# One attention and mixture kernel: float16 state products in every batch, keys scaled into a spare tile, weight words fetched a step early, products of a chunk pair three side steps later

## The chip, the cores and the metric

One core of one Trainium2 chip runs the whole program. The metric is device time in microseconds, from the program's start to its end. The kernel before took 1023.17 us in the median of three runs (1021.74 to 1024.06). Everything about time in this text comes from those runs and from one profiled execution of 1023.83 us.

## The reference

Four batches, 768 positions, 384 features (8 heads of 48). Three stages follow each other:

```python
# 1. attention: per head a complex decay a, normalised to a length under 1
a = a * min(|a|, 0.999) / (|a| + 1e-6)
S[t] = a[t] * S[t-1] + k[t] v[t]^T           # complex state, 48 x 48 per head
y[t] = q[t] . Re(S[t])
# 2. first feed-forward layer
u = x + (U V applied along the sequence)      # rank 32
x = u + relu(u @ w1) @ w2                     # 384 -> 1536 -> 384
# 3. second feed-forward layer
u = x + Re(fft over sequence and features of x)
un = layernorm(u)
x = u + relu(un @ w1') @ w2'
```

All results are float32, and the kernel keeps near that precision by splitting operands: a product of float32 accuracy is made of three products of a high and a low part (high x high, high x low, low x high).

## The kernel before, in words

**Attention.** A batch is cut into six chunks of 128 positions, taken in three pairs. `decays` and `turns` work elementwise on a pair (logarithm, running sums, sine and cosine) and write for each chunk a tile `QK` of turned queries and keys, position on the partitions. Six DMAs on SP's queue (L427) carry `QK` to `QT`, feature on the partitions. `products` then works on a chunk in small steps: the scores `sc` from `QT` (L452, TensorE, float32), the masked scores `pm` (VectorE, L457), the transposes `kp` of the keys from `QK` (L466), their split into `kh` and `kl` (L475, L476), the sum `y` (L484), the state's increment `g` (L484), and the new state `S` (L563 to L583). `g` is the product of keys and values of the chunk; `S` is scaled by `fe`, the decay over the chunk.

Two kinds of chunk exist. In the plain ones (all of batch 0, the first four of batch 1) keys are copied whole into `ke` (ScalarE, L471), and `y` and `g` are float32 products; `g` takes 16 products of 128 x 64 and 128 x 32 weights, 32 instructions in the profile. In the others values and keys are split into float16 parts (`vh`, `vl`, `kh`, `kl`), and `g` is 24 float16 products. In those chunks the keys are scaled by the decay before they are transposed: three in-place activations on `QK` (L509), after the DMAs have read it.

**First layer.** `moe_units(0)` goes over 4 batches x 2 groups of 384 positions x 12 slices `f` of the hidden features. A slice is nine products into `hp` (L92 to L94), `hh` on ScalarE (L179), the low part `hl` on VectorE (L181), and nine products into `acc`, those for the slice before. The weights come as 64-bit words: `load_w` fetches them (`stw`, L120), ScalarE and VectorE rebuild float32 numbers (`wxw`, L109 to L127) and split them (`w`, L138, L139).

**What runs beside what.** Attention of batch 0 stands alone, with the weights of the first layer woven in (`first_attention`). While batch b is in the first layer, `Side(attention(b+1), total, 40)` does the steps of the next batch's attention: 40 side slots share `total` steps evenly. In `attention`, each pair's products run zipped with the elementwise steps of the next pair. The second layer (`moe_units(1)`) follows with the Fourier part beside it.

**Order.** The program hands instructions to a scheduler that lays each engine's own order down by modelled readiness and by priority (`urgent`, `tc.high_priority`); on the chip each engine then goes strictly in its order. `warm` (L1001) are products whose result nobody uses, put behind given instructions: 20 behind the first scores, 4 behind the first and 4 behind the last of the products into `z`.

Of the kernel before, what the change touches and what calls it, by code (L numbers as in the profile page):

```python
# [23 lines left out]
NC = 6  # L24
# [10 lines left out]
IM_MOST = 0.96  # L35

# [6 lines left out]
def mixer_kernel(ctx, tc, a_in, qk_in, v_in, u_in, v4_in, w_in, cc_in, ss_in, cb_in, sb_in, id_in, mask_in, rows_in, out):  # L43
# [69 lines left out]
    def from_f64(src, name):  # L113
# [5 lines left out]
        st = moe.tile([128, 384, 2], I32, tag="u", name=f"st{name}", bufs=5)[:, :n]  # L119
        nc.sync.dma_start(st.rearrange("p n w -> p (n w)"), src.bitcast(I32))  # L120
# [11 lines left out]
    def load_w(mi, f, z):  # L132
# [4 lines left out]
        x = from_f64(w_in[mi, f][:, zs], f"w{mi}_{f}_{z}")  # L137
# [119 lines left out]
    def decays(m):  # L257
# [4 lines left out]
        def mk(nm):  # L262
            return at(f"{nm}{b}_{cc[0]}")

        if b == 0:
            if m == 2:
                turn = at(f"turn{b}_{cc[0]}", "turn", 1, (128, 2, 3, 2, 128))
                s1, s2 = turn[:, 0], turn[:, 1]
            else:
                s1, s2 = mk("L"), mk("s")  # L270
            T_ = a[:, 1]
            qf, kf = qk[:, 0], qk[:, 1]
        else:
            turn = at(f"turn{b}_{cc[0]}", "turn", 1, (128, 2, 3, 2, 128))
            T_, s1, s2 = turn[:, 1], mk("L"), mk("s")
# [5 lines left out]
        ew[m] = T_, Th, qf, kf, ends, a if b == 0 else turn  # L281
# [90 lines left out]
    def turns(m):  # L372
# [3 lines left out]
        T_, Th, qf, kf, ends, turn = ew[m]  # L376
# [6 lines left out]
        for js in jj:  # L383
# [31 lines left out]
            for j in range(js.start, js.stop):  # L415
# [12 lines left out]
                qkt[b, c] = QT, QK  # L428
                yield

    def products(m, j):
# [11 lines left out]
        QT, QK = qkt[b, c]  # L443
# [19 lines left out]
        def turned(z):  # L463
            kp.append(bank(f"kp{n}_{z}", pool)[:, :384])
            for i in range(3):
                T.transpose(kp[z][:, i * 128 : (i + 1) * 128], QK[:, z, i, 128:256], ident)  # L466

        def split(z):
            src = kp[z].rearrange("t (x h) -> t h x", h=8)
            if plain:  # L470
                A.copy(ke[:, :, z, :], src)  # L471
                return
            dh = kh[:, :768].rearrange("t (h z x) -> t h z x", h=8, z=2)[:, :, z, :]
            dl = kl[:, :768].rearrange("t (h z x) -> t h z x", h=8, z=2)[:, :, z, :]
# [29 lines left out]
        if not last:
            fe = t3("fe", 2, (96, 8))
            G.tensor_scalar(fe, QT[:, :, 256], 1.0 if plain and c == 0 else 1.0 / FSCALE, 0.0, ALU.mult, ALU.add)
            if not plain:
                for i in range(3):
                    A.activation(QK[:, :, i, 128:256], QK[:, :, i, 128:256], AF.Copy, scale=QK[:, 0, i, 256:257])  # L509
# [749 lines left out]
```

## Time and profile before

| | |
|---|---|
| runs, median of 3 | 1023.17 us (1021.74 to 1024.06) |
| profiled execution | 1023.83 us |
| its span | 1022.1 us |
| mean granted TensorE clock | 0.944 |
| TensorE products / VectorE / ScalarE / GpSimd busy | 86% / 64% / 46% / 23% |

The profile is of one execution. PE is TensorE (products), PEld its weight loads, DVE VectorE, ACT ScalarE, POOL GpSimd, SP the engine whose queue issues the DMAs. A granted clock of 1.00 is 2.4 GHz and of 0.50 is 1.2 GHz. By the first `hh` (L179) of each batch the span falls into: attention of batch 0 up to 147.4 us; first layer of batch 0 to 319.9, of batch 1 to 453.1, of batch 2 to 575.6, of batch 3 to 681.2; second layer to the end.

### The profile page before, as it was taken

How to read it: one execution, taken by the hardware profiler on the slowest of the kernel's cores; microseconds unless marked ns; L12 is line 12 of the kernel's file. 1: busy time of each engine (PE TensorE's matmuls, PEld its weight loads, DVE VectorE, ACT ScalarE, POOL GpSimd, SP SyncE). 2: the span in 40 equal slices, each digit the busy share in tenths (PEclk: the TensorE clock that was granted, in tenths of full speed). 3: DMA queues.
4: the chain of work that ended last, by engine and by line, in shares of the span. 5: the costliest groups of instructions: out<-in, count | busy, mean ns of one | idle time of the engine just before them, and what ended most of it. 6: DMA issues, size and time to landing. Idle time of an engine off the chain costs nothing.

```text
span 1022.1 us, 16249 instructions
## 1 busy us (share of the span) xinstructions
PE 878.7 (86%) x6338; PEld 832.0 (81%) x6338; DVE 651.0 (64%) x1117; ACT 465.3 (46%) x880; POOL 232.2 (23%) x249
## 2 busy tenths in 40 slices
PE   0069857989877987969989999789999999999997
PEld 0057647978867887959989999689999999999997
DVE  7965987747768695876964728996544545362121
ACT  7435557566766877676743223353212212222111
POOL 5312552311101011120204306633312222010000
PEclk9996959889897998989989999999999999999999
DMA  9069438273562527347065104342101011000000
GB/s 350 0 86 147 157 124 140 101 125 77 80 104 87 75 72 123 78 86 110 9 86 201 41 1 120 121 148 62 63 18 45 24 55 47 1 25 24 1 24 27
DMA packets 47094, 83.40 MB, mean 82 GB/s; under 512 B 5600, under 2 KB 36064, under 8 KB 47008
## 3 DMA queue, kind: packets, MB, share of 16 engines
q1 hardware_dynamic: 45152, 75.96, 32.5%
q0 software_dynamic: 1856, 6.31, 1.8%
q8 instruction: 52, 0.85, 0.4%
q14 instruction: 34, 0.28, 0.1%
HBM read 53.79 MB, written 9.44 MB: 62 GB/s over the span
## 4 chain that ended last, share of the span: by engine, by line
PE 54%; DVE 20%; DMA 12%; SPq 4%; issue 4%; ACT 4%; POOL 2%; DVEq 0%; ACTq 0%; POOLq 0%
DMA QT<-QK 8%; PE acc L94 7%; PE acc L92 7%; PE hp L92 7%; PE hp L93 7%; PE hp L94 7%; PE acc L93 7%; PE sc L452 4%; SPq L427 4%; DMA stw<-in_w_dram 3%; PE g L484 2%; PE y L484 2%; DVE QK L423 1%; DVE ph L461 1%; DVE wxw L126 1%
## 5 line engine op out<-in xcount | busy, mean ns | idle before, releaser
L181 DVE SCALAR_TENSOR_TENSOR hl<-hp,hh 128x384 fp32r<-128x384 f32 x192 | 105.4, 552 | 195.4 <-ACT hh L179 195.1
L179 ACT ACTIVATE hh<-hp 128x384 fp32r<-128x384 f32 x192 | 93.3, 488 | 284.3 <-PE hp L94 265.8
L92 PE MATMUL acc<-w,hh 128*128 128x384 f32 x576 | 201.1, 349 | 7.9 <-ACT hh L179 7.9
L93 PE MATMUL acc<-w,hh 128*128 128x384 f32 x576 | 195.3, 339 | 0.0
L94 PE MATMUL acc<-w,hl 128*128 128x384 f32 x576 | 161.2, 349 | 11.9 <-DVE hl L181 11.8
L92 PEld LDWEIGHTS acc<-w,hh 128*128 128x128 f32 x576 | 109.8, 191 | 12.0 <-ACT hh L179 10.8
L94 PEld LDWEIGHTS acc<-w,hl 128*128 128x128 f32 x576 | 105.0, 193 | 16.3 <-DVE hl L181 16.1
L93 PEld LDWEIGHTS acc<-w,hh 128*128 128x128 f32 x576 | 109.8, 191 | 0.0
L92 PE MATMUL hp<-u,w 128*128 128x384 f32 x288 | 101.1, 356 | 5.4 <-ACT u L661 5.4
L93 PE MATMUL hp<-u,w 128*128 128x384 f32 x288 | 102.1, 355 | 3.1 <-DVE u L662 3.1
L94 PE MATMUL hp<-u,w 128*128 128x384 f32 x288 | 101.1, 352 | 0.0
L93 PE MATMUL hp<-n,w 128*128 128x384 f32 x288 | 96.5, 335 | 1.4 <-DVE n L947 1.2
L92 PE MATMUL hp<-n,w 128*128 128x384 f32 x288 | 96.4, 335 | 0.0
L94 PE MATMUL hp<-n,w 128*128 128x384 f32 x288 | 96.4, 335 | 0.0
L452 PE MATMUL sc<-QT 96*128 96x128 f32 x384 | 67.8, 336 | 29.7 <-DMA QT<-QK 19.6
L452 PEld LDWEIGHTS sc<-QT 96*128 96x128 f32 x384 | 61.5, 240 | 34.8 <-issue 28.8
L139 POOL TENSOR_TENSOR w<-wxw,w 128x384 fp32r<-128x384 f32 x48 | 57.1, 1196 | 80.1 <-ACT w L138 80.0
L466 PE MATMUL kp<-ident,QK 128*128 128x128 f32 x120 | 21.9, 306 | 49.3 <-DVE QK L423 49.3
L92 PEld LDWEIGHTS hp<-u,w 128*128 128x128 f32 x288 | 57.0, 200 | 6.8 <-ACT u L661 6.7
L93 PEld LDWEIGHTS hp<-u,w 128*128 128x128 f32 x288 | 57.3, 199 | 4.8 <-DVE u L662 4.7
L466 PEld LDWEIGHTS kp<-ident,QK 128*128 128x128 f32 x120 | 17.1, 160 | 50.4 <-DVE QK L423 49.3
L94 PEld LDWEIGHTS hp<-u,w 128*128 128x128 f32 x288 | 57.3, 199 | 0.2
(314 smaller groups left out, 1816.9 us busy)
## 6 DMA issues: line engine op xcount, KB each, us to landing
QT<-QK SPq DMA_DIRECT2D x144, 129.0 KB, 5.6
stw<-in_w_dram SPq DMA_DIRECT2D x48, 384.0 KB, 3.3
ain<-in_a_dram SPq DMA_DIRECT2D x12, 768.0 KB, 4.4
qkin<-in_qk_dram SPq DMA_DIRECT2D x12, 768.0 KB, 4.7
x1d<-x SPq DMA_DIRECT2D x24, 192.0 KB, 4.1
vin<-in_v_dram SPq DMA_DIRECT2D x18, 192.0 KB, 2.7
lo<-x1d SPq DMA_DIRECT2D x12, 192.0 KB, 2.9
out_dram<-lo SPq DMA_DIRECT2D x12, 192.0 KB, 1.9
```

Of the source, the lines that this page charges most:

```text
L92: T.matmul(o, ah, bh, start=start, stop=False, skip_group_check=skip)
L93: T.matmul(o, ah, bl, start=False, stop=False, skip_group_check=skip)
L94: T.matmul(o, al, bh, start=False, stop=stop, skip_group_check=skip)
L126: V.scalar_tensor_tensor(out=xi, in0=xi, scalar=3, in1=low, op0=ALU.logical_shift_left, op1=ALU.bitwise_or)
L139: G.tensor_tensor(w[:, 1, zs], x, f32(w[:, 0, zs]), ALU.subtract)
L179: A.activation(hh, hp, AF.Relu)
L181: V.scalar_tensor_tensor(out=hl, in0=hp, scalar=0.0, in1=f32(hh), op0=ALU.max, op1=ALU.subtract)
L423: V.tensor_tensor(QK[:, :, :, to], x[:, :, j].unsqueeze(1).to_broadcast([128, 2, 3, 128]), w, ALU.mult)
L427: nc.sync.dma_start(QT[p0 : p0 + 16], QK[:, z, i, :])
L452: T.matmul(ps[:, h, :], q[:, 128:256], q[:, :128], start=True, stop=True)
L466: T.transpose(kp[z][:, i * 128 : (i + 1) * 128], QK[:, z, i, 128:256], ident)
L484: T.matmul(out[p, hsl], l(h)[:, p], r[:, hsl], start=h == 0 and o == 0, stop=h == 7 and o == len(ops) - 1, skip_group_check=True,)
```

## The change

1. **States.** `g` is made of float16 halves in the plain chunks too: values are split into `v` halves (ScalarE and VectorE), keys into `k` halves (the copy on ScalarE stays, one VectorE instruction per half of the features is added), and `g` takes 24 float16 products; the last head reads 96 columns, so the cleared tails of `kh` and `kl` go. The old state is scaled by `fe` before `g` is there, and one VectorE instruction (ScalarE for the first chunk) finishes the new state.
2. **Scaled keys.** For every chunk but the last, three activations write the scaled keys into a tile that is dead by then (`scaled`: the input tile in batch 0, `ls` in the others), and `kp` transposes from there. They stand where `QK` has just been made, not behind its DMAs. `L` and `s` become one tile `ls`.
3. **Weight words.** `weights` fetches the words of the next step before it works on those of this one.
4. **Lag.** `LAG = 3`: the products of the second and third pair come three side steps later against the elementwise steps, and the steps to share rise from 58, 48 and 48 to 61, 51 and 51 over the same 40 slots.
5. **Warm products.** From 20, 4 and 4 to 20, 36 and 20: the 36 behind the last product into `z`, the 20 behind those into `zv`.
6. `fe` is made one step later, always with the same factor.

```diff
+LAG = 3
     def weights(mi):
-        for f in range(FB):
-            for z in range(2):
-                load_w(mi, f, z)
-                yield
+        todo = [(f, z) for f in range(FB) for z in range(2)]
+        st = None
+        for at, (f, z) in enumerate(todo):
+            now = fetch(*words(mi, f, z)) if st is None else st
+            st = fetch(*words(mi, *todo[at + 1])) if at + 1 < len(todo) else None
+            load_w(mi, f, z, now)
+            yield
...
+                if c != NC - 1:
+                    for i in range(3):
+                        A.activation(scaled[:, :, i, j], QK[:, :, i, 128:256], AF.Copy, scale=ends[:, i, j : j + 1])
                 for z in range(2):
...
-                T.transpose(kp[z][:, i * 128 : (i + 1) * 128], QK[:, z, i, 128:256], ident)
+                T.transpose(kp[z][:, i * 128 : (i + 1) * 128], scaled[:, z, i], ident)
...
-            if plain:
-                A.copy(ke[:, :, z, :], src)
-                return
...
+            vs = slot(f"v{n}").bitcast(F16).rearrange("p (z m) -> p z m", z=2)
+            vh, vl = vs[:, 0], vs[:, 1]
+        if not (plain and last):
             A.activation(vh, vin, AF.Copy, scale=VSCALE)
             V.scalar_tensor_tensor(out=vl, in0=vin, scalar=VSCALE, in1=vh, op0=ALU.mult, op1=ALU.subtract)
-            if not plain:
-                for i in range(3):
-                    A.activation(QK[:, :, i, 128:256], QK[:, :, i, 128:256], AF.Copy, scale=QK[:, 0, i, 256:257])
...
-                summed(gp, 96, [(lambda h: kf[:, h * 96 : h * 96 + 96], vin)])
-                    V.scalar_tensor_tensor(out=sS, in0=gp[:96], scalar=FSCALE, in1=S, op0=ALU.mult, op1=ALU.add)
-                    (G if b == 0 else V).tensor_tensor(sh, sh, f3, ALU.mult)
+            if S is not None:
+                (G if b == 0 else V).tensor_tensor(sh, pS.rearrange("p (h e) -> p h e", h=8), f3, ALU.mult)
+            hs = lambda x: lambda h: ks[:, x + h * 96 : x + min(h * 96 + 128, 1536 - x)]
+            summed(gp, [(hs(0), vh), (hs(0), vl), (hs(768), vh)])
...
-        for i in range(3):
-            m = 3 * b + i
-            yield from zipped(both(m), elementwise(m + 1))
+        m = 3 * b
+        ahead = chain(*(elementwise(m + 1 + i) for i in range(3)))
+        yield from zipped(chain(padded(both(m), 16 + LAG), padded(both(m + 1), 16), both(m + 2)), ahead)
...
-    for after, n in zip(scored[:1] + ends, [20, 4, 0, 0, 0, 0, 4]):
+    for after, n in zip(scored[:1] + ends, [20, 36, 0, 0, 0, 20]):
...
-                side = Side(attention(b + 1), (58, 48, 48)[b], 40)
+                side = Side(attention(b + 1), (58 + LAG, 48 + LAG, 48 + LAG)[b], 40)
```

VectorE, batch 0, from the reduction of chunk 1's angle (L404 before, L410 after) to the masked scores of chunk 0. `v_1` and `v_2` are halves of values, `k_0` halves of keys, `QK_1` the turned queries and keys of chunk 1. Before:

```order
L404 SCALAR_TENSOR_TENSOR ain_0_112<-ain_0_112 128x768
L408 COPY cy_1_240<-ain_0_112 128x3
L419 COPY QK_3_338<-fe_2_151 128x6x2
L423 TENSOR_TENSOR QK_1_245<-qkin_0_118,ain_0_112 128x6x128 x2
L388 TENSOR_TENSOR ain_2_114<-ain_2_114,cy_1_240 128x3
L457 TENSOR_TENSOR pm_0_283<-sc_0_0_284,mask 128x512
```

After:

```order
L511 SCALAR_TENSOR_TENSOR v_1_348<-vin_0_126,v_1_348 128x384
L410 SCALAR_TENSOR_TENSOR ain_0_112<-ain_0_112 128x3x128
L511 SCALAR_TENSOR_TENSOR v_2_498<-vin_0_126,v_2_498 128x384
L481 SCALAR_TENSOR_TENSOR k_0_313<-kp_0_0_314,k_0_313 128x8x48
L414 COPY cy_1_241<-ain_0_112 128x3
L481 SCALAR_TENSOR_TENSOR k_0_313<-kp_0_1_320,k_0_313 128x8x48
L425 COPY QK_3_351<-fe_2_149 128x6x2
L429 TENSOR_TENSOR QK_1_246<-qkin_0_118,ain_0_112 128x6x128 x2
L466 TENSOR_TENSOR pm_0_287<-sc_0_0_288,mask 128x512
```

Four instructions that split values and keys now stand ahead of the `QK_1` pair, two of them (`k_0`) behind transposes of chunk 0.

TensorE, first layer of batch 0, where the first scores of batch 1 (`sc_0_0`, reading `QT_0`) stand among the slices; `hp_0_0_8` is slice 8's hidden product, `acc` the output. Before:

```order
L94 MATMUL hp_0_0_7_1469<-u_0_2_994,w_7_1036 128x384
L92 MATMUL acc_0_0_0_1124<-w_6_966,hh_0_0_6_1419 128x384
L93 MATMUL acc_0_0_0_1124<-w_6_966,hh_0_0_6_1419 128x384
L92 MATMUL acc_0_0_1_1125<-w_6_966,hh_0_0_6_1419 128x384
L93 MATMUL acc_0_0_1_1125<-w_6_966,hh_0_0_6_1419 128x384
L92 MATMUL acc_0_0_2_1126<-w_6_966,hh_0_0_6_1419 128x384
L93 MATMUL acc_0_0_2_1126<-w_6_966,hh_0_0_6_1419 128x384
L452 MATMUL sc_0_0_1198<-QT_0_1091 128x128 x4
L452 MATMUL sc_0_1_1232<-QT_0_1091 128x128 x4
L466 MATMUL kp_0_0_1273<-ident,QK_0_1089 128x128 x3
L94 MATMUL acc_0_0_0_1124<-w_6_966,hl_0_0_6_1421 128x384
```

After:

```order
L95 MATMUL acc_0_0_2_1263<-w_6_1047,hl_0_0_6_1594 128x384
L93 MATMUL hp_0_0_8_1716<-u_0_0_1042,w_8_1212 128x384
L94 MATMUL hp_0_0_8_1716<-u_0_0_1042,w_8_1212 128x384
L95 MATMUL hp_0_0_8_1716<-u_0_0_1042,w_8_1212 128x384
L93 MATMUL hp_0_0_8_1716<-u_0_1_1067,w_8_1212 128x384
L94 MATMUL hp_0_0_8_1716<-u_0_1_1067,w_8_1212 128x384
L95 MATMUL hp_0_0_8_1716<-u_0_1_1067,w_8_1212 128x384
L93 MATMUL hp_0_0_8_1716<-u_0_2_1073,w_8_1212 128x384
L94 MATMUL hp_0_0_8_1716<-u_0_2_1073,w_8_1212 128x384
L95 MATMUL hp_0_0_8_1716<-u_0_2_1073,w_8_1212 128x384
L461 MATMUL sc_0_0_1335<-QT_0_1222 128x128 x4
L461 MATMUL sc_0_1_1370<-QT_0_1222 128x128 x3
```

The scores stood between slice 7's hidden products and the last third of slice 6's `acc`; now they stand behind slice 8's hidden products, twelve products of the layer later.

SP's queue, end of batch 0's attention: `stw_f_z` are fetches of weight words, `QT_4` and `QT_5` the six DMAs each of the last two chunks. Before:

```order
L120 DMA stw_0_1_561<-in_w_dram 128x768
L120 DMA stw_1_0_654<-in_w_dram 128x768
L427 DMA QT_4_394<-QK_4_392 16x8x258 x6
L427 DMA QT_5_426<-QK_5_424 16x8x258 x6
L226 DMA ain_2_456<-in_a_dram 128x1536
L120 DMA stw_1_1_663<-in_w_dram 128x768
L120 DMA stw_2_0_755<-in_w_dram 128x768
```

After:

```order
L117 DMA stw_0_1_595<-in_w_dram 128x768
L117 DMA stw_1_0_605<-in_w_dram 128x768
L436 DMA QT_4_414<-QK_4_412 16x8x258 x6
L117 DMA stw_1_1_710<-in_w_dram 128x768
L117 DMA stw_2_0_720<-in_w_dram 128x768
L436 DMA QT_5_456<-QK_5_454 16x8x258 x6
L238 DMA ain_2_486<-in_a_dram 128x1536
```

Two fetches have moved ahead of the six DMAs of chunk 5.

## Rows read from the trace of the kernel before

**Rows 1.** The page: engines' busy time; chain that ended last, by line.

```profile
PE 878.7 (86%) x6338; PEld 832.0 (81%) x6338; DVE 651.0 (64%) x1117; ACT 465.3 (46%) x880; POOL 232.2 (23%) x249
...
DMA QT<-QK 8%; PE acc L94 7%; PE acc L92 7%; PE hp L92 7%; PE hp L93 7%; PE hp L94 7%; PE acc L93 7%; PE sc L452 4%; SPq L427 4%; DMA stw<-in_w_dram 3%; PE g L484 2%; PE y L484 2%; DVE QK L423 1%; DVE ph L461 1%; DVE wxw L126 1%
```

**Rows 2.** Stages: length, PE, PEld, DVE, ACT, POOL busy (count), clock, DMA share, GB/s.

```profile
49.30:147.40 98.10, 73.60 (x704) 58.38 (x704) 73.21 (x107) 47.53 (x94) 33.21 (x27) 0.83 0.61 126
147.40:319.90 172.50, 147.20 (x1092) 134.99 (x1093) 118.72 (x176) 114.90 (x205) 32.98 (x27) 0.86 0.52 105
...
681.20:1022.00 340.80, 333.62 (x2011) 328.66 (x2010) 150.79 (x333) 73.53 (x157) 55.49 (x73) 0.99 0.11 34
```

**Rows 3.** TensorE in time: start, duration, work, [idle before]: one g of either kind.

```profile
71.48 3.65 PE L484 MATMUL g<-vin,ke 128*64 128x48 f32 x32
...
342.49 0.37 PE L484 MATMUL g<-vh,kh 128*128 128x48 f16 x8
...
343.10 0.42 PE L92 MATMUL acc<-w,hh 128*128 128x384 f32 x1
```

**Rows 4.** Groups by line: out<-in, count, busy us, mean ns, idle before and releaser.

```profile
L509 ACT ACTIVATE QK<-QK 128x256 f32<-128x256 f32 x33 | 16.4, 504 | 24.5 <-DMA QT<-QK 24.3
L476 DVE SCALAR_TENSOR_TENSOR kl<-kp,kh 128x384 f16<-128x384 f32 x22 | 11.6, 544 | 1.8 <-ACT kh L475 1.8
L502 DVE SCALAR_TENSOR_TENSOR vl<-vin,vh 128x384 f16<-128x384 f32 x14 | 7.7, 552 | 7.9 <-PE g L484 7.9
```

**Rows 5.** Waits of VectorE from 49.3 to 147.4: us, times, longest.

```profile
DVE QK L419 <- DMA QT<-QK: 10.3, 3, 4.0
DVE S L565 <- PE g L484: 9.2, 2, 6.3
```

**Rows 6.** Waits of TensorE from 147.4 to 575.6: us, times, longest.

```profile
PE sc L452 <- DMA QT<-QK: 11.2, 4, 4.6
PE acc L92 <- ACT hh L179: 7.5, 8, 1.9
PE g L484 <- DVE kl L476: 4.2, 2, 2.5
```

**Rows 7.** TensorE in time: five first scores of a pair, with the wait.

```profile
179.11 0.76 PE L452 MATMUL sc<-QT 96*128 96x128 f32 x2 [4.57 <-DMA QT<-QK]
...
216.51 0.76 PE L452 MATMUL sc<-QT 96*128 96x128 f32 x2 [2.02 <-DMA QT<-QK]
...
312.34 2.08 PE L452 MATMUL sc<-QT 96*128 96x128 f32 x8 [0.80 <-DVE u L662]
...
390.94 0.76 PE L452 MATMUL sc<-QT 96*128 96x128 f32 x2 [4.55 <-issue]
...
523.30 0.55 PE L452 MATMUL sc<-QT 96*128 96x128 f32 x1 [3.46 <-DMA QT<-QK]
```

**Rows 8.** Three stretches at half clock, columns as in rows 2.

```profile
130.20:154.10 23.90, 14.68 (x40) 12.08 (x41) 20.20 (x34) 13.65 (x27) 12.80 (x9) 0.50 0.42 133
178.00:184.80 6.80, 5.69 (x24) 5.72 (x25) 2.59 (x6) 4.55 (x8) 2.34 (x4) 0.50 0.56 212
522.80:529.60 6.80, 6.30 (x26) 6.24 (x27) 3.65 (x5) 2.33 (x4) 0.20 (x1) 0.50 1.13 165
```

**Rows 9.** TensorE in time: warm products, and the end of batch 0's attention.

```profile
67.03 2.24 PE L1001 MATMUL warm<-ident,mask 128*128 128x256 f16 x19
...
132.22 1.33 PE L650 MATMUL zv<-vst,zst 128*128 128x384 f32 x3 [5.24 <-DVE zst L620]
136.39 1.01 PE L92 MATMUL hp<-u,w 128*128 128x384 f32 x2 [2.84 <-ACT u L661]
```

**Rows 10.** All waits of the program: ScalarE on weight words.

```profile
ACT wxw L109 <- DMA stw<-in_w_dram: 31.9, 24, 2.7
```

**Rows 11.** VectorE in time, then GpSimd, around 123 us.

```profile
122.90 4.59 DVE L362 COPY fe<-L 128x6 f32<-128x6 f32 x1
...
124.59 1.81 POOL L367 TENSOR_TENSOR s<-qkin,s 128x768 f32<-128x768 f32 x1
```

More of the change, by code (lines that the diff above doesn't have):

```diff
@@ L111, in kept, with fetch @@
             fn(*args, **kw)
-    def from_f64(src, name):
+    def fetch(src, name):
         n = src.shape[-1]
@@ L375, in turns @@
         at = attention_pool()
-        T_, Th, qf, kf, ends, turn = ew[m]
+        T_, Th, qf, kf, ends, turn, scaled = ew[m]
         use(TRIG)
@@ L482, in summed @@
                     hsl = slice(h * 48, (h + 1) * 48)
-                    for p in (slice(0, 64), slice(64, rows)) if plain else (slice(0, 128),):
+                    for p in (slice(0, 64), slice(64, 128)) if halves else (slice(0, l(h).shape[-1]),):
                         T.matmul(
@@ L498, in products @@
         scored.append(nc.cur_bb.bb.instructions[-1])
-        if not plain:
+        if b == 0 and not last:
+            vs = slot(f"v{n}").bitcast(F16).rearrange("p (z m) -> p z m", z=2)
+            vh, vl = vs[:, 0], vs[:, 1]
+        elif b:
             vh, vl = t3("vh", 2, (128, DM), F16), t3("vl", 1, (128, DM), F16)
+        if not (plain and last):
             A.activation(vh, vin, AF.Copy, scale=VSCALE)
             V.scalar_tensor_tensor(out=vl, in0=vin, scalar=VSCALE, in1=vh, op0=ALU.mult, op1=ALU.subtract)
+        if not plain:
             ph, plo = t3("ph", 1, (128, 2, 8, 128), F16).rearrange("p s h t -> s p h t")
[L504 to L507, printed above, removed]
-                for i in range(3):
-                    A.activation(QK[:, :, i, 128:256], QK[:, :, i, 128:256], AF.Copy, scale=QK[:, 0, i, 256:257])
         yield
@@ L519, in products @@
         if not last:
-            if not plain:
-                kh, kl = t3("kh", 1, (128, 8 * 96 + 32), F16), t3("kl", 1, (128, 8 * 96 + 32), F16)
-                G.memset(kh[:, 768:], 0.0)
-                G.memset(kl[:, 768:], 0.0)
-            elif b == 0:
-                ke = moe.tile([128, 8, 2, 48], F32, tag="u", name=f"ke{n}", bufs=5)
-            else:
-                ke = at(f"ke{n}", "ph", 1, (128, 1024), pl=attp[1])[:, :768].rearrange("p (h z x) -> p h z x", h=8, z=2)
+            if b == 0:
+                ks = moe.tile([128, 1536], F16, tag="u", name=f"k{n}", bufs=5)
+            else:
+                ks = t3("k", 1, (128, 1536), F16)
+            kh, kl = ks[:, :768], ks[:, 768:]
             turned(0)
@@ L533, in products @@
             split(1)
+            fe = t3("fe", 2, (96, 8))
+            G.tensor_scalar(fe, QT[:, :, 256], 1.0 / FSCALE, 0.0, ALU.mult, ALU.add)
         load_v(b, c + 1)
@@ L575, in products @@
         yield
-        if not last and not plain:
+        if not last:
+            scale = 1.0 / (KSCALE * VSCALE) if plain else GSCALE
             if S is None:
-                A.activation(sS, gp[:96], AF.Copy, scale=GSCALE)
+                A.activation(sS, gp[:96], AF.Copy, scale=scale)
             else:
-                V.scalar_tensor_tensor(out=sS, in0=gp[:96], scalar=GSCALE, in1=sS, op0=ALU.mult, op1=ALU.add)
-            shi, slo = t3("Sh", 1, (96, DM), F16), t3("Sl", 1, (96, DM), F16)
-            A.copy(shi, sS)
-            V.tensor_tensor(slo, sS, shi, ALU.subtract)
-            state[b] = sS, shi, slo
+                V.scalar_tensor_tensor(out=sS, in0=gp[:96], scalar=scale, in1=sS, op0=ALU.mult, op1=ALU.add)
+            state[b] = sS
+            if not plain:
+                shi, slo = t3("Sh", 1, (96, DM), F16), t3("Sl", 1, (96, DM), F16)
+                A.copy(shi, sS)
+                V.tensor_tensor(slo, sS, shi, ALU.subtract)
+                state[b] = sS, shi, slo
         yield
```

51 lines of the change are left out of this document (20 added, 31 removed).

## The prediction

> **What bounds the kernel now.** I read the page first. TensorE is busy 86% of the span, VectorE 64%. In the chain that ended last the layers' six lines of products (L92 to L94) have 42% and the transfers from QK to QT 8%, the largest single entry [rows 1]. So most of the time is products, but a good part is waiting for what attention hands over. The table of stages says where: from 49.3 to 147.4 us, where attention of batch 0 stands alone, TensorE is busy 73.6 of 98.1 us and VectorE 73.2; in the first layer of batch 0 (147.4 to 319.9) TensorE is busy 147.2 of 172.5, a share of 0.85, at a granted clock of 0.86 [rows 2]. In the alone stretch neither engine is full, because they wait for each other: VectorE stands 10.3 us for QK's transfers and 9.2 us for g [rows 5]. In the layers beside attention TensorE's own list of waits has 11.2 us for QT, four times, and 4.2 us for kl, twice [rows 6]. What follows such a wait is the second half of its price: 178.0 to 184.8 us, right behind the 4.57 us wait at 179.11, and 522.8 to 529.6, at the 3.46 us wait of 523.30, run at half clock, 1.2 GHz [rows 7, 8]. The second layer is not touched by the change.
>
> **States.** One plain g is 32 instructions in 3.65 us; the float16 one is 24 in 0.61 us (343.10 less 342.49) [rows 3]. That is 3.04 us less, for nine chunks 27.4 us of TensorE: 15.2 in batch 0, 12.2 in the first layer of batch 0. Added are 18 splits of keys at 0.544 and nine of values at 0.552 on VectorE, 14.8 us, and nine copies of values on ScalarE [rows 4]. In batch 0 that is ten key and five value splits, and one value split for batch 1 done early: 16 times 0.55, 8.8 us. VectorE there has 24.9 us idle (98.1 less 73.2) [rows 2], and 9.2 of that is the very wait for g [rows 5], which goes with it. From the order, the four splits ahead of QK_1 stand where VectorE until now stood for QK's DMAs (4.0 us at the longest [rows 5]), so they are hidden; if the cover were gone they would cost 2.2. The later ones are not. The gain of 9.2 and the cost of 8.8 nearly meet; bounds are -9.2 (all splits in gaps) and +8.8 (no wait shrinks). I take -2, since some splits do fall into gaps. In the first layer of batch 0 TensorE is the engine nearest its limit: 0.85 of 12.2 is 10.4; the eight key and four value splits there are 6.6 us of VectorE, with the low parts hl queued behind them. VectorE is busy 118.7 of 172.5 [rows 2], so I charge a third, 2 us. That makes -8; bounds -12.2 and -3.8 (all 6.6 in series).
>
> **Warm products.** Today zv waits 5.24 us for VectorE and the first hp 2.84 us for ScalarE [rows 9], and 130.2 to 154.1 is at half clock with TensorE busy 14.7 us [rows 8]. A warm product took 0.118 us (2.24 by 19) [rows 9]; 36 are 4.2 us and fit into the first wait, 20 are 2.4 and fit into the second. If they keep the clock at 2.4 GHz, half of the 14.7 us, 7.3, goes; but 9.2 us of that stretch are waits for other engines, which a faster TensorE only lengthens. If the clock had dropped anyway, 36 would take 8.5 and push zv by 3.3. Bounds -7.3 and +3.3; I take -3, a little beyond their middle, because the two waits are where the clock falls.
>
> **Lag.** I counted on TensorE's order how many of the layer's products stand between the turned keys on VectorE and the first scores. The second layer does 96 slices of 18 products in 340.8 us at a clock of 0.99 [rows 2], so one is 0.19 us as an estimate from above, and 0.38 at half clock. Batch 1's first chunk gets 12 more, 2.3 to 4.6 us against its 4.57 us wait: -3, and with half of what the half clock costs there (5.69 by two by two, 1.4) -4. Batch 3's chunk 4 gets 29 more, 5.5 us, against 3.46: the wait goes, and half of 6.30 by two, 1.6, with it: -5. Batch 2's chunk 2 gets 18 more; no row here gives its wait, so I put it at -1.5, below 2.02, the least wait of those in [rows 7] that QT ends. Batch 1's chunk 2 loses six, so its 2.02 us wait grows by 1. Batch 2's chunk 4 keeps its 27 and its 4.55. Batch 2's chunk 0 loses 36, because its keys are turned two slices later; its scores were held by u and not by QT [rows 7], at a change of batch where TensorE stands anyway, so I charge 0.5, at most the 4.55 of the nearest. Sum -9; bounds 0 (the wait only moves to the next thing that is late) and -16 (all 11.2 us [rows 6], and the 4.5 us that the half clock cost).
>
> **Scaled keys.** 33 activations at 0.504 become 60, +13.6 us of ScalarE, of which 27 are in chunks that had none [rows 4]. What goes is the stand of ScalarE for QT before the old ones, 24.3 us in all [rows 4]; of that TensorE saw the 4.2 us for kl [rows 6], since kp no longer stands behind the DMAs. Queued behind the new activations are the hh of the layer; TensorE's wait for hh is 7.5 us in eight today [rows 6], and a trio is 1.5 us. I take -3 for kl and +1 for hh: -2; bounds -4.2 and +7.5 (that wait doubled). The shared tile ls must wait for the transposes of the pair two before; TensorE has long done them in the order, so I charge nothing; the bound is one trio of steps, 2 us.
>
> **Weight words.** ScalarE stands 31.9 us for weight words, 24 times [rows 10], nearly all where it is not the bound. Fetching ahead takes little of the first layer's start, -1. On SP's queue two fetches move ahead of chunk 5's six DMAs, and the second needs a buffer that VectorE frees only after the first words are decoded. If it is late, chunk 5 and the start of the layer are late; I bound it by the longest word wait, 2.7 us [rows 10], and take 0.
>
> **Sum.** -2 -8 -3 -9 -2 -1 = -25 on the profiled execution of 1023.8, so 998.8; the median of the runs is 0.7 lower, which gives 998.
>
> **A rule against it.** The value split reads two operands from SBUF. A copy of six columns on VectorE took 4.59 us while GpSimd worked through operations of up to 1.81 us [rows 11]. The Trainium skill, page SBUF — State Buffer, section "SBUF: two separate sides", says that VectorE and GpSimd share a port pair as an exclusive lock, which a VectorE operation with two SBUF inputs contends for against a GpSimd operation that reads SBUF, whichever starts first holding it to its end. The trace agrees with waiting of that kind, though it doesn't name the cause. By the rule each of the nine value splits could stand for one such operation, 16 us of VectorE more in the worst case; the sum above holds none of it, because the 14 present value splits average 0.552 us [rows 4].
>
> **The rivals.**
> The waits only move: TensorE's stands for QT are shared by the DMAs and VectorE's pace, and a later score only makes pm, kp and y late. For it: QT is waited for at several places, and 4.55 stays in any case [rows 7]. Against: the waits are isolated, between stretches of full work. Then the lag's -9 is 0: 1008.
> More goes: all waits of rows 6 for QT and kl, the half-clock stretches behind them and the full 7.3 of the start. Lag -16, warm -7, states -14, scaled keys -4, words -1: 42 less, 982. Against: VectorE is near full just before the first layer.
> Nothing: the faster g is eaten by VectorE in both stretches (-10 becomes 0), and the rest balances: 1022 to 1024. Against: 0.85 of TensorE's time in the larger stretch is busy.
> Slower: VectorE becomes the bound from 49 to 320 us. Its 14.8 us of splits are then in series, QK and with it QT come that much later, so that the lag gives nothing; only the 9.2 us for g are saved: 1023.8 + 14.8 - 9.2, 1029. It decides once VectorE has no idle time left in those 270 us; today it has 24.9 and 53.8 [rows 2], which speaks against it.
>
> **How the numbers follow.** Forecast (988 to 1003) 0.47; waits only move 0.25; more goes 0.13; nothing 0.07; slower 0.08. About 0.2%, 2 us, is what a measurement of this kernel can tell from no change. Faster: 0.47 + 0.25 + 0.13, 0.85; of "nothing" 0.05 is the same and 0.02 slower, so slower is 0.10. The range leaves out the two last cases and the far end of "more goes", and reaches beyond 1008 by the 10 us that the bounds of warm products, ScalarE and SP's queue add: 978 to 1018.
>
> **What would show it.** Right: g in the plain chunks at about 0.6 us; VectorE's wait for g from 49 to 147 gone; first hp of the layer at 2.4 GHz; no wait at the first scores of batch 3's chunk 4, under 2 us at batch 1's first chunk; kl out of TensorE's waits; each stage shorter, the second layer unchanged. Wrong: the stage before the first hh as long as now with VectorE full; new waits of TensorE for hh, pm or ph of the size of those removed; a wait of batch 2's first scores for QT of several microseconds; zv started later than now after the last z.

## The result and the profile after

The changed kernel takes 1010.01 us in the median of nine runs (1006.54 to 1013.38), the kernel before 1021.74 in nine runs beside it (1016.05 to 1025.73): a ratio of 0.987, 95% interval 0.984 to 0.990; the medians lie 11.7 us apart, 1.1%. A second comparison gave 1010.77 us and 0.991 (0.988 to 0.994). The forecast was 998, so the direction was right and the size about half; 1010 lies outside the forecast's own 988 to 1003, inside the whole range of 978 to 1018, and nearest to the rival in which the waits only move (1008). It is near that rival by number alone: that rival has the lag at nothing and the states in the first layer at their full 8 us, and the stages below look more like the other way round.

The profiled execution of the changed kernel has a span of 1008.1 us. First the table of its stages (length, busy time of TensorE, weight loads, VectorE, ScalarE, GpSimd, then granted clock, DMA share, GB/s), cut at the first `hh` of each batch, from the alone stage to the second layer:

```profile
49.30:143.40 94.10, 67.55 (x715) 56.98 (x716) 78.73 (x121) 56.58 (x116) 30.93 (x25) 0.86 0.68 131
143.40:317.80 174.40, 140.13 (x1084) 129.33 (x1083) 127.73 (x186) 118.81 (x217) 33.14 (x25) 0.86 0.52 104
317.80:447.20 129.40, 114.70 (x969) 110.32 (x966) 103.15 (x155) 96.36 (x179) 17.16 (x11) 0.93 0.48 93
447.20:558.50 111.30, 106.30 (x958) 102.73 (x958) 81.51 (x135) 63.59 (x127) 25.56 (x26) 0.98 0.44 97
558.50:667.30 108.80, 99.16 (x593) 94.05 (x592) 79.88 (x165) 38.25 (x79) 40.57 (x45) 0.98 0.28 87
667.30:1008.10 340.80, 333.61 (x2011) 328.60 (x2009) 150.08 (x333) 73.67 (x157) 55.90 (x73) 0.99 0.11 34
```

and the kernel before, for the three layers that were not shown:

```profile
319.90:453.10 133.20, 116.05 (x999) 110.75 (x998) 101.28 (x153) 97.29 (x179) 20.09 (x21) 0.95 0.47 90
453.10:575.60 122.50, 111.79 (x957) 107.54 (x953) 88.06 (x146) 64.87 (x126) 30.09 (x36) 0.94 0.42 88
575.60:681.20 105.60, 96.40 (x587) 91.72 (x586) 75.10 (x154) 36.10 (x77) 37.48 (x42) 1.00 0.29 89
```

Against [rows 2] the alone stage lost 4.0 us, the layer of batch 1 lost 3.8, those of batches 2 and 3 together 8.0 (228.1 to 220.1), and the second layer nothing. The layer of batch 0, where most was forecast, got 1.9 us longer. TensorE is busy 7.1 us less there (147.2 to 140.1) and idle 9.0 us more (25.3 to 34.3), while VectorE is busy 9.0 us more. The saving is real; it became idle time.

What TensorE waits for in that layer (us, times, longest), then what VectorE stands for there:

```profile
PE acc L95 <- DVE hl L193: 9.7, 4, 3.7
PE y L489 <- ACT ph L469: 5.4, 2, 4.4
PE sc L461 <- ACT ls L89: 4.1, 1, 4.1
```

```profile
DVE S L563 <- POOL fe L536: 10.5, 2, 5.4
```

The wait for hl was 2.9 us in the same layer before, and that for ph 0.4:

```profile
PE acc L94 <- DVE hl L181: 2.9, 2, 1.9
```

Most of the wait for ph is one of 4.44 us at the layer's end. ScalarE makes ph only after it has stood 4.64 us for QT, to make `qh` (the high part of a query tile), and has done 3.9 us of other work behind that. ScalarE, then TensorE:

```profile
310.34 1.05 ACT L519 CAST qh<-QT 96x1024 f16<-96x1024 f32 x1 [4.64 <-DMA QT<-QK]
```

```profile
315.91 0.34 PE L489 MATMUL y<-vh,ph 128*128 128x48 f16 x4 [4.44 <-ACT ph L469]
```

The third row is put down to ScalarE, but the transfers show what it is: SP issues the twelve DMAs of batch 1's second pair from 207.36 on, and the scores and, on GpSimd, `fe` start together when QT is there. From the timelines of TensorE, GpSimd and SP:

```profile
217.16 3.75 PE L461 MATMUL sc<-QT 96*128 96x128 f32 x16 [4.07 <-ACT ls L89]
```

```profile
217.19 0.20 POOL L536 TENSOR_SCALAR fe<-QT 96x8 f32<-96x8 f32 x1 [19.52 <-DMA QT<-QK]
```

```profile
207.36 9.21 SPq L436 DMA_DIRECT2D QT<-QK  x12
```

This is the 2.02 us wait of [rows 7], 4.07 us here. In the profiled execution of the second comparison the same scores start at nearly the same time, but the products ahead of them end later and the wait is 1.70 us, so the growth is not a firm one:

```profile
216.79 2.77 PE L461 MATMUL sc<-QT 96*128 96x128 f32 x16 [1.70 <-DMA QT<-QK]
```

In all, TensorE's waits for QT in this layer fell, from 7.8 to 5.3 us with the misnamed row counted in; those for hl and ph grew. The float16 g itself is as fast as forecast where the granted clock is 1.00: 24 products between 224.91 and 225.54, 0.63 us, against 3.65 [rows 3]:

```profile
224.91 0.37 PE L489 MATMUL g<-vh,k 128*128 128x48 f16 x8
225.12 0.36 PE L489 MATMUL g<-vl,k 128*128 128x48 f16 x8
225.32 0.38 PE L489 MATMUL g<-vh,k 128*128 128x48 f16 x8
225.54 0.60 PE L93 MATMUL hp<-u,w 128*128 128x384 f32 x2
```

### The profile page after: what moved, and what is told of

It is laid out like the page before. It is cut to its first block, busy times and chain, and to the rows that moved or that the text cites. A ratio compares the mean times of both kernels' runs of the same rounds, so it can differ in the third digit from the quotient of the medians.

```text
span 1008.1 us, 16236 instructions
## 1 busy us (share of the span) xinstructions
PE 861.5 (85%) x6318; PEld 822.0 (82%) x6318; DVE 664.9 (66%) x1142; ACT 478.7 (47%) x918; POOL 226.1 (22%) x227
## 4 chain that ended last, share of the span: by engine, by line
PE 45%; DVE 27%; DMA 9%; ACT 7%; issue 5%; SPq 2%; POOL 2%; DVEq 0%; ACTq 0%; POOLq 0%
PE acc L95 6%; PE hp L93 6%; PE acc L93 6%; PE hp L95 6%; PE hp L94 6%; PE acc L94 6%; DMA QT<-QK 5%; DMA stw<-in_w_dram 3%; SPq L436 2%; PE sc L461 2%; DVE wxw L133 2%; DVE QK L429 2%; DVE hl L193 1%; DVE wxw L132 1%; DVE ls L353 1%
## 5 line engine op out<-in xcount | busy, mean ns | idle before, releaser
L95 PE MATMUL acc<-w,hl 128*128 128x384 f32 x576 | 162.2, 347 | 20.5 <-DVE hl L193 20.3
L95 PEld LDWEIGHTS acc<-w,hl 128*128 128x128 f32 x576 | 104.8, 192 | 25.5 <-DVE hl L193 25.3
L93 PEld LDWEIGHTS acc<-w,hh 128*128 128x128 f32 x576 | 110.8, 192 | 10.7 <-ACT hh L191 9.1
L461 PE MATMUL sc<-QT 96*128 96x128 f32 x384 | 64.8, 328 | 28.1 <-DMA QT<-QK 12.3
L148 POOL TENSOR_TENSOR w<-wxw,w 128x384 fp32r<-128x384 f32 x48 | 55.0, 1154 | 62.4 <-ACT w L147 62.1
L536 POOL TENSOR_SCALAR fe<-QT 96x8 f32<-96x8 f32 x20 | 7.4, 372 | 222.2 <-DMA QT<-QK 216.4
L94 PEld LDWEIGHTS hp<-n,w 128*128 128x128 f32 x288 | 54.1, 188 | 2.0 <-DVE n L943 2.0
```

Source lines behind the costliest of these rows:

```text
L93: T.matmul(o, ah, bh, start=start, stop=False, skip_group_check=skip)
L94: T.matmul(o, ah, bl, start=False, stop=False, skip_group_check=skip)
L95: T.matmul(o, al, bh, start=False, stop=stop, skip_group_check=skip)
L461: T.matmul(ps[:, h, :], q[:, 128:256], q[:, :128], start=True, stop=True)
```

## The experiments

Every kernel was timed in five rounds beside the kernel before. One thing has to be said ahead. Each edit, however small, also makes the scheduler lay the engines' instructions down in another order; only one (the ninth) leaves every instruction in its place. So a difference below is the part taken out *and* the order that came with it. The first four experiments ran on one chip, the next four and the last four on two others; the kernel before took 1023.1, 1022.1 and 1023.3 us beside them. The stages in the table (us) are those of one profiled execution of each: the alone stage, the layers of batches 0 and 1, and those of 0 and 1 and of 2 and 3 together.

| kernel | median | ratio to before (95%) | alone | 0 | 1 | 0+1 | 2+3 |
|---|---|---|---|---|---|---|---|
| before | 1021.7 | | 147.4 | 172.5 | 133.2 | 305.7 | 228.1 |
| changed | 1010.0 | 0.987 (0.984 to 0.990) | 143.4 | 174.4 | 129.4 | 303.8 | 220.1 |
| changed again (e5) | 1010.8 | 0.991 (0.988 to 0.994) | 143.4 | 173.0 | 131.2 | 304.2 | 219.8 |
| no lag (e1) | 1013.9 | 0.994 (0.991 to 0.997) | 143.2 | 162.9 | 139.4 | 302.3 | 224.3 |
| old warm products (e2) | 1020.4 | 1.001 (0.998 to 1.004) | 145.3 | 166.0 | 136.5 | 302.5 | 224.2 |
| float32 g (e3) | 1013.7 | 0.993 (0.990 to 0.997) | 148.4 | 171.6 | 130.3 | 301.9 | 221.9 |
| no low parts in batch 1 (e4) | 1009.5 | 0.990 (0.986 to 0.994) | 143.2 | 168.8 | 141.5 | 310.3 | 214.1 |
| before with new warm products (e6) | 1031.8 | 1.011 (1.007 to 1.016) | 147.9 | 174.1 | 136.9 | 311.0 | 229.9 |
| old fetch of words (e7) | 1016.5 | 0.996 (0.993 to 0.998) | 142.0 | 168.5 | 144.2 | 312.7 | 217.2 |
| scaling behind the scores (e8) | 1021.1 | 1.000 (0.997 to 1.003) | 143.9 | 167.2 | 140.4 | 307.6 | 223.6 |
| without the 20 (e9) | 1011.7 | 0.988 (0.983 to 0.993) | 143.5 | 174.0 | 132.1 | 306.1 | 220.5 |
| 35 for 36 (e10) | 1020.1 | 0.999 (0.995 to 1.002) | 144.4 | 167.2 | 140.3 | 307.5 | 225.2 |
| 33 for 36 (e11) | 1019.5 | 0.995 (0.992 to 0.998) | 143.8 | 166.9 | 139.7 | 306.6 | 223.1 |
| fe on GpSimd (e12) | 1016.0 | 0.996 (0.993 to 1.000) | 143.7 | 169.8 | 137.1 | 306.9 | 223.9 |

The columns 0 and 1 have to be read together. In eight variants (e1, e2, e4, e7, e8, e10, e11, e12) the layer of batch 1 is 7.1 to 14.8 us longer than in the changed kernel, but that of batch 0 is 4.6 to 11.5 shorter, and the sum differs by -1.5 to +8.9. With one or three idle products less (e10, e11) this happens too, so a shorter layer of batch 0 alone says nothing of the part taken out.

**No lag.**

```diff
-LAG = 3
+LAG = 0
```

> The changed kernel with LAG = 0. Theory 'lag': the first layer of batch 2 became 11.1 us shorter because the scores of batch 3's chunk 4 stand 29 layer products later; with LAG 0 they stand at 39 products behind their keys again, and the wait of 3.5 us with the half clock behind it comes back: batch 2's layer +5 to +10 us, the program 1014 to 1020. Rival 'order in general': the schedule was shaken up by all parts, and the lag alone is worth nothing: within 2 us of 1010.

3.9 us more than the changed kernel, below the expected 4 to 10. Batches 2 and 3 lose 4.2 us of their 8.0 but keep 3.8, and the layers of 0 and 1 are 1.5 us shorter. The lag may carry half of the gain in the late layers; the rest is not its work. The wait of 3.5 us that was to come back at batch 3's chunk 4 comes back as 1.88, against 0.56 in the changed kernel. At batch 1's first chunk, where the lag was to cover a wait of 4.57 us, the kernel without it waits 1.48 us; the changed kernel first, then this one:

```profile
174.35 1.80 PE L461 MATMUL sc<-QT 96*128 96x128 f32 x14 [1.17 <-DMA QT<-QK]
```

```profile
172.92 2.02 PE L461 MATMUL sc<-QT 96*128 96x128 f32 x16 [1.48 <-DMA QT<-QK]
```

So most of the gain at that place is not the lag's.

**Old warm products.**

```diff
-    for after, n in zip(scored[:1] + ends, [20, 36, 0, 0, 0, 20]):
+    for after, n in zip(scored[:1] + ends, [20, 4, 0, 0, 0, 0, 4]):
```

> The changed kernel with the old warm products (20, 4 and 4). Theory 'warm': the alone stage (to the first hh) gained 4.0 us mostly from the clock, so it gets 3 to 5 us longer, and the first hp run at half clock: 1013 to 1015. Rival 'states': the gain is that of the float16 g, the old warm products cost under 1 us: 1010 to 1011.

The program loses the whole gain, 10 us, but the alone stage only 1.9. Both theories miss: the warm products do not do that by their clock in the alone stage. The profiled execution, the fastest of the twelve (1015.7), lost 5.8 us: 1.9 in the alone stage, 4.1 in the layers of batches 2 and 3 and 1.0 in the second layer. The layers of 0 and 1 together are 1.3 us shorter, although one wait of 10.7 us stands at the end of batch 1's (below).

**Float32 g.**

```diff
...
-            summed(gp, [(hs(0), vh), (hs(0), vl), (hs(768), vh)])
+            if plain:
+                kf = ks.bitcast(F32)
+                summed(gp, [(lambda h: kf[:, h * 96 : h * 96 + 96], vin)], halves=True)
+            else:
+                summed(gp, [(hs(0), vh), (hs(0), vl), (hs(768), vh)])
...
```

> The changed kernel with float32 products for g in the plain chunks, and without the splits of values and keys there (27 VectorE instructions less, 27 us more of TensorE). Theory 'VectorE and the hand-over pace the first layer of batch 0': that stage (174.4 us) stays within 2 us although TensorE is busy 12 us more in it, its waits for hl (9.7 us) fall by half; the alone stage gets 2 to 5 us longer; in all 1010 to 1016. Rival 'TensorE paces it, something else ate the gain': the stage gets 8 to 12 us longer, the alone stage 2 to 5, in all 1020 to 1027.

1013.7, in the first theory's span and far from the rival's 1020. The layer of batch 0 in this kernel, and TensorE's wait for hl in it:

```profile
148.40:320.00 171.60, 144.01 (x1092) 129.97 (x1093) 121.09 (x174) 117.72 (x215) 31.51 (x25) 0.87 0.52 106
```

```profile
PE acc L95 <- DVE hl L193: 4.8, 4, 2.1
```

TensorE is busy 3.9 us more than in the changed kernel (I had expected 12), VectorE 6.6 less, the wait for hl has halved, and the layer is 2.8 us shorter, not longer. Why the rest of TensorE's work took less here was not taken apart. The four layers together are 523.8 us here and 523.9 there. So no gain of the float16 states shows in the layers; that the new order hides one of a few us is not ruled out, since orders alone move these layers by 6 to 9 us (e11, e10). In the alone stage the difference is 5.0 us (148.4 against 143.4), more than the other variants of the changed kernel differ there (142.0 to 145.3).

**No low parts in batch 1's plain chunks.**

```diff
+            if not (plain and b == 1):
                 V.scalar_tensor_tensor(out=dl, in0=src, scalar=KSCALE, in1=dh, op0=ALU.mult, op1=ALU.subtract)
...
+            kv = [(hs(0), vh)] if plain and b == 1 else [(hs(0), vh), (hs(0), vl), (hs(768), vh)]
+            summed(gp, kv)
```

> The changed kernel without the low parts of values and keys in batch 1's plain chunks (left out: 12 VectorE splits of 0.55 us, and g there is 8 products instead of 24). Theory 'VectorE paces the first layer of batch 0': the stage gets 4 to 7 us shorter, in all 1003 to 1006. Rival 'the hand-over of QT and the order pace it, VectorE has room': under 2 us shorter, 1008 to 1010.

The layer of batch 0 is 168.8 us, 5.6 shorter, as the theory of VectorE's pace has it. That does not show it: with all splits in place and one or three idle products less the layer is 167.2 and 166.9 us (e10, e11). The program is not faster, 1009.5, which lies in the rival's span. Batch 1's layer is 141.5 us, 12.1 longer, with a single wait of 7.8 us of the kind that the tenth experiment shows. Which theory holds stays open.

**The changed kernel again.**

> The changed kernel once more, as the anchor for the kernels beside it. Theory: the ratio to the kernel before is that of the first comparison, 0.984 to 0.990, 1006 to 1013 us. Rival (the first comparison was a lucky placing on one chip): 0.990 to 0.996, near the kernels of the first experiments.

Median 1010.8 against 1010.0: the same kernel comes out the same, while the ratio moved by 0.4%. By its time the theory's span has it, by its ratio, 0.991, the rival's; the runs of the kernel before, on which the ratio rests too, spread more than those of this one (1009.3 to 1011.7). From here on I compare medians of the changed kernel's variants, and hold under 3 us for nothing.

**The kernel before with the new warm products.**

```diff
-    for after, n in zip(scored[:1] + ends, [20, 4, 0, 0, 0, 0, 4]):
+    for after, n in zip(scored[:1] + ends, [20, 36, 0, 0, 0, 20]):
```

> The kernel before with the new list of warm products only. Theory 'warm carries much of the gain': taking the warm products out of the changed kernel cost 1.4% in the ratios, so adding them alone gives 1010 to 1015. Rival 'they only help where the rest of the change has made the alone stage tight': 1018 to 1022, as forecast (-3).

Slower by 1.1%, outside both expectations. TensorE in time around the first hp:

```profile
135.68 0.79 PE L650 MATMUL zv<-vst,zst 128*128 128x384 f32 x3 [1.41 <-DVE zst L620]
144.03 0.69 PE L92 MATMUL hp<-u,w 128*128 128x384 f32 x1 [4.39 <-ACT u L661]
```

The warm products fill the wait for zst, but u and hp come 7.6 us later than in [rows 9], and the first hh no earlier (147.9). The 10 us lie in all stages (5 of them in the layers of batches 0 and 1, 2 in the second layer), and no one wait makes them; how they come about stays open.

**Old fetch of weight words.**

```diff
-            now = fetch(*words(mi, f, z)) if st is None else st
-            st = fetch(*words(mi, *todo[at + 1])) if at + 1 < len(todo) else None
-            load_w(mi, f, z, now)
+            load_w(mi, f, z)
```

> The changed kernel without the fetch of weight words a step ahead. Theory 'words are worth about 1 us': within 3 us of the anchor. Rival 'the early words start the first layer sooner, and so carry the 4 us of the alone stage': 3 to 6 us more than the anchor, with the first hh 3 us later.

6 us more, but the first hh comes 1.4 us *earlier* (142.0), so the rival's reason is wrong too. The layer of batch 0 is also shorter, 168.5; the loss is in batch 1's layer (144.2 against 129.4). The two together are 8.9 us longer, those of 2 and 3 are 2.9 shorter.

**Scaling behind the scores.**

```diff
-                        A.activation(scaled[:, :, i, j], QK[:, :, i, 128:256], AF.Copy, scale=ends[:, i, j : j + 1])
...
+        if not last:
+            for i in range(3):
+                A.activation(scaled[:, :, i], QK[:, :, i, 128:256], AF.Copy, scale=QK[:, 0, i, 256:257])
         yield
```

> The changed kernel with the three scaling activations put back behind the scores, where they wait for QT, still into the spare tile. Theory 'the early scaling takes kl out of the path' (-2 forecast): 2 to 5 us more than the anchor, TensorE's wait for k in g back at 3 to 5 us. Rival 'the added activations cost as much as they give': within 2 us of the anchor or less.

10 us more, twice what I expected at most. TensorE's wait for k in g, to be back at 3 to 5 us, is 3.5 (2.6 in the changed kernel). Batch 1's layer is 11 us longer (140.4), but that of batch 0 is 7.2 shorter: of the 7.9 us between the profiled executions 3.8 lie in these two layers, 3.5 in the two behind them. So the wait for k does not carry the loss.

**Without the 20 behind zv.** The same order on every engine.

```diff
-[20, 36, 0, 0, 0, 20]
+[20, 36, 0, 0, 0, 0]
```

> The changed kernel without the 20 warm products behind zv; every other instruction stands in the same place on every engine. Theory 'the clock at the first hp': they fill the wait of hp for u and keep the clock up, so that without them the first hh comes 1 to 3 us later and the program takes 1012 to 1015. Rival 'no worth by themselves, what cost 1% in the second experiment was the order that came with the old list': 1009 to 1011, with the stages behind unchanged.

1011.7, 0.9 to 1.7 us over the two medians of the changed kernel, and the first hh comes at 143.5 against 143.4. Over 128 to 150 us, first the changed kernel, then this one:

```profile
128.00:150.00 22.00, 15.81 (x83) 13.32 (x81) 21.69 (x34) 14.71 (x27) 11.38 (x9) 0.84 0.36 110
```

```profile
128.00:150.00 22.00, 12.91 (x51) 10.77 (x52) 21.41 (x34) 14.11 (x26) 11.53 (x9) 0.69 0.38 109
```

The clock is up, 0.84 against 0.69, and it buys nothing that can be told from the noise: VectorE is busy 21.7 of the 22 us, so a faster TensorE has little to gain there. The rival holds in kind, though 1011.7 is 0.7 us above its span; the first hh is not the 1 to 3 us later that the theory needs.

**One warm product less, and three less.**

```diff
-[20, 36, 0, 0, 0, 20]
+[20, 35, 0, 0, 0, 20]
```

> The changed kernel with 35 instead of 36 warm products behind z: 0.12 us less work, but the scheduler lays some 40% of TensorE's products of the first layer down in another order. Theory 'the order that falls out is worth several microseconds by itself, and the effects of single parts hold it': 1014 to 1022, with the first layers of batches 0 and 1 changed by several microseconds each. Rival 'the parts themselves cause the differences': 1009 to 1012.

> The changed kernel with 33 instead of 36 warm products behind z: 0.35 us less work, and a third order. Theory 'order': anywhere from 1004 to 1022, not equal to the one with 35, and over 3 us from 1010. Rival 'parts': 1009 to 1012.

10.1 and 9.5 us slower than the first median of the changed kernel, with 0.12 and 0.35 us less of work that nobody needs. Beside the ninth experiment, which has the changed kernel's order and ran on the same chip, it is 8.4 and 7.8 us, and no run of either (1015.9 to 1025.1) comes near one of it (1009.7 to 1013.2). Order by itself is worth nearly as much as the whole measured gain. One place where it acts can be shown, the end of batch 1's layer. ScalarE and TensorE in the changed kernel:

```profile
429.58 0.47 ACT L615 CAST zst<-z 128x384 fp32r<-128x384 f32 x1
436.67 1.04 ACT L519 CAST qh<-QT 96x1024 f16<-96x1024 f32 x1 [5.14 <-DMA QT<-QK]
```

```profile
438.15 0.69 PE L93 MATMUL acc<-w,hh 128*128 128x384 f32 x1 [3.43 <-ACT hh L191]
```

and with 35 warm products:

```profile
434.83 1.04 ACT L519 CAST qh<-QT 96x1024 f16<-96x1024 f32 x1 [5.49 <-DMA QT<-QK]
436.52 0.46 ACT L615 CAST zst<-z 128x384 fp32r<-128x384 f32 x1
```

```profile
441.53 1.01 PE L646 MATMUL xp<-vst,zst 128*128 128x384 f32 x2 [10.52 <-DVE zst L616]
```

`zst` is on the path to the next batch's u. `qh` waits for QT. Where `zst` stands ahead of it on ScalarE, the wait costs 3.4 us through hh; where it stands behind, 10.5. With 33 warm products hh and `zst` both stand behind `qh`, and TensorE waits 5.14 us for hh:

```profile
435.82 1.04 ACT L519 CAST qh<-QT 96x1024 f16<-96x1024 f32 x1 [5.23 <-DMA QT<-QK]
438.62 0.46 ACT L615 CAST zst<-z 128x384 fp32r<-128x384 f32 x1
```

The same spot in the other traces: of the eight variants with a longer layer of batch 1, four (e2, e4, e7, e10) have `zst` behind `qh` and TensorE waits 7.8 to 10.7 us for it; the other four (e1, e8, e11, e12) wait 4.4 to 5.8 for hh or u behind the same `qh`. In the kernel with float32 g, whose order has `zst` and the last hh ahead of `qh` there, TensorE waits 3.85 us for u behind it. This place is not the whole loss, and in the sum of the layers it is hardly seen: with 35 warm products the layer of batch 1 is 10.9 us longer and that of batch 0 7.2 shorter, and of the 9.7 us between the profiled executions 1.0 lie in the alone stage, 3.7 in the layers of 0 and 1 and 5.1 in those of 2 and 3. How these orders lose the rest was not taken apart.

**The old state scaled on GpSimd.**

```diff
-                (G if b == 0 else V).tensor_tensor(sh, pS.rearrange("p (h e) -> p h e", h=8), f3, ALU.mult)
+                G.tensor_tensor(sh, pS.rearrange("p (h e) -> p h e", h=8), f3, ALU.mult)
```

> The changed kernel with the old state scaled by fe on GpSimd in batches 1 to 3 too, not on VectorE. Theory 'VectorE stands behind fe, which waits for QT (22.9 us in five waits), and holds hl and pm behind it': TensorE's waits for hl fall from 20 to under 14 us and the program takes 1002 to 1007. Rival 'TensorE waits for the same QT meanwhile': VectorE's wait moves to pm, 1008 to 1013.

VectorE no longer waits for `fe` (22.9 us in the changed kernel). Its waits for the scores and for `qh`, both made from QT, took that over; the changed kernel, then this one:

```profile
DVE pm L466 <- PE sc L461: 11.4, 11, 1.8
DVE ql L520 <- ACT qh L519: 7.2, 2, 4.1
```

```profile
DVE pm L466 <- PE sc L461: 27.8, 15, 5.0
DVE ql L520 <- ACT qh L519: 19.6, 5, 5.9
```

TensorE's waits for hl are 17.5 us, hardly fewer than 20.3, and the time is 1016. The rival is right in kind: both engines stand for the same QT. The expected 1008 to 1013 was too low, and how much of the excess is order is not known.

## Why the prediction was right and wrong

**States in the first layer (forecast -8; the stage with all parts in it came out 1.9 us longer, 0.5 in the second profile).** The step "0.85 of 12.2 is 10.4" failed. That TensorE is busy 85% of a stage does not mean that 85% of what it saves comes off the stage. The saving turned into waits, for hl (2.9 to 9.7 us) and ph (0.4 to 5.4) above all, which VectorE and ScalarE set. With float32 g the four layers take as long. With the lag's -4 and +1 the sum had this stage at -11; that it did not come is about as much as the whole forecast was off (25 forecast, 14.0 between the profiled executions).

**Value splits on VectorE (forecast 0.552 us each).** The nine that the change adds took 0.61 in the mean, one of them 1.11. The rest of the excess fell on splits that were there before: the 18 of batches 1 to 3 take 0.857 in the mean, where the 14 before took 0.552 [rows 4]; the key splits take 0.546. The excess, 18 times 0.305, is 5.5 us, of which the sum held nothing; the prediction's worst case held 16. Its reason for nothing, the mean of the 14, failed: none of those had run beside a GpSimd operation that reads SBUF tiles, and in the new order some do, five of which have all of the excess (last section).

**States and warm products in the alone stage (forecast -2 and -3, measured -4.0 together).** The sum is near, its division was not. Float32 g gives 5.0 of it back, the old warm products 1.9, the 20 behind zv 0.1. The splits on VectorE fell into gaps, as the lower bound had it: its wait for g went from 9.2 to 1.3 us and its idle time from 24.9 to 15.4. The 36 warm products did not fit in the profiled execution. They took 6.25 us, not 4.2, at a granted clock of 0.63, and zv started behind them at 128.65, though its zst was there at 126.6. In the ninth experiment, with the same order, and in the second profile of the changed kernel they took 4.09 us and zv started at 126.78 and 126.63. The changed kernel, then the ninth:

```profile
122.64 6.25 PE L997 MATMUL warm<-ident,mask 128*128 128x256 f16 x36
```

```profile
122.09 4.09 PE L997 MATMUL warm<-ident,mask 128*128 128x256 f16 x36
```

The first hp came at 133.35 and 133.49, so neither the push nor the clock moved it.

**Lag.** The waits at the places came about as forecast: 1.17 us for 4.57 at batch 1's first chunk, 0.56 for 3.46 at batch 3's chunk 4, none at batch 2's first. The cause was not the one forecast, or only in part: without the lag the first two are 1.48 and 1.88. Batch 1's chunk 2, put at 1 us more, had 2.05 more in one profile and 0.32 less in the other. Batch 2's chunk 4, said to keep its 4.55, waited 2.74, and batch 3's chunk 2 1.74 where it had 0.97. The layers of 2 and 3 gained 8.0 us, forecast 6; without the lag 3.8 stays. Two sums are off: 340.8 us by 96 times 18 products is 0.197 us, not 0.19, and the half clock in the upper bound costs 6.0 us by its rows, not 4.5. Neither moves the forecast.

**Scaled keys.** The step "what goes is the stand of ScalarE for QT, 24.3 us" failed. ScalarE's next instruction that reads QT took the wait over:

```profile
ACT qh L519 <- DMA QT<-QK: 19.8, 5, 5.7
ACT qh L519 <- issue: 5.8, 2, 3.1
```

25.6 us (the second row too ends with QT, the two are what ScalarE waits for it in all), in seven pieces where there had been eighteen; one of 5 us at a time then stands in front of hh, zst or ph. TensorE's wait for kl, 4.2 us, became one of 2.6 for k, where -3 was put; its wait for hh did not grow (7.5 to 5.1). Before, qh stood 4.5 us in all, and for y, since the scaling ahead of it had done the waiting for QT.

**Weight words (forecast -1).** Nothing of it is shown: ScalarE stands 31.0 us for words where it stood 31.9, and without the early fetch the first hh came 1.4 us earlier.

**Sum and order.** The parts do not add. Taking single parts out costs 3.9, 10.4, 3.7, 6.4 and 11.1 us against 1010, 35.5 together, where all of them made 12. Two orders of the changed kernel that differ in nothing but one or three idle products give ratios of 0.999 and 0.995. So this much is shown: the change in the order in which it was measured is about 1% faster (0.987 and 0.991). How much of that is its parts and how much the order is not settled; the alone stage (2 to 5 us, but for float32 g) and the layers of 2 and 3 (3 to 14 us) were shorter than before in every variant of the changed kernel, those of 0 and 1 in none by more than 4. No variant that holds qh back on purpose was tried, and none beat the changed kernel beyond the noise.

## What to carry to other kernels

When a queue's instruction stops waiting for a transfer, look for the next reader of that transfer on the same queue and for what stands behind it, since the wait goes there. Do not charge a stage with its busiest engine's share: find the round that ends it, and ask whether the saved engine already idles in that round. And where a scheduler writes the order, first time the kernel with a change of nothing, such as one idle product less; a part's effect means something only above that.

## What the runs showed of the hardware

Five value splits, which read two SBUF tiles, got slow beside GpSimd; key splits, which read PSUM and one SBUF tile, did not. From the groups of the changed kernel (busy us, mean ns):

```profile
L481 DVE SCALAR_TENSOR_TENSOR k<-kp,k 128x384 f16<-128x384 f32 x40 | 21.6, 546 | 2.4 <-ACT k L480 2.4
L511 DVE SCALAR_TENSOR_TENSOR vl<-vin,vh 128x384 f16<-128x384 f32 x18 | 15.4, 857 | 2.5 <-PE g L489 2.5
```

and one of the five slow ones in time, VectorE and then GpSimd:

```profile
241.18 2.12 DVE L511 SCALAR_TENSOR_TENSOR vl<-vin,vh 128x384 f16<-128x384 f32 x1
```

```profile
239.74 3.15 POOL L373 TENSOR_TENSOR ls<-qkin,ls 128x768 f32<-128x768 f32 x1 [13.92 <-DVE ls L367]
```

The split starts inside the GpSimd operation and ends 0.4 us behind it, and hl and acc wait behind it (acc 2.20 us at 244.36). All five (1.11 to 2.14 us) start inside such an operation and end 0.4 us behind it, at the same places in the second profile of the kernel. In one of them a key split ran inside the same GpSimd operation, just ahead of the value split, and took its usual time. VectorE, then GpSimd:

```profile
451.24 0.53 DVE L481 SCALAR_TENSOR_TENSOR k<-kp,k 128x384 f16<-128x384 f32 x1
452.15 1.22 DVE L511 SCALAR_TENSOR_TENSOR vl<-vin,vh 128x384 f16<-128x384 f32 x1
```

```profile
449.80 3.16 POOL L373 TENSOR_TENSOR ls<-qkin,ls 128x768 f32<-128x768 f32 x1 [11.07 <-PE y L489]
```

The trace agrees with the Trainium skill, SBUF — State Buffer, section "SBUF: two separate sides", by the rule that the prediction quotes. A sixth value split, at 122.53, took 0.54 us inside a GpSimd record of 5.62 us. By the 1.81 us that the shortest such operation took [rows 11], its own work would lie behind the split; that is an estimate.

The other surprise is the spread. Nine runs of the changed kernel lie between 1006.5 us at a mean granted clock of 0.953 and 1013.4 us at 0.940, with the others between, roughly in the order of their clock. In the last comparison most runs of the kernel before lie between 1013.0 us (0.953) and 1028.7 (0.933).
